# Layer 1's first stage: k of tiles 2 to 15 and q of six of them by seven block products per pair of token tiles

## The chip, the cores and the metric

One Trainium2 chip, one of its cores. The metric is the device time of one execution in microseconds; the median of the runs of a kernel counts. All arithmetic is fp32, done on TensorE in three passes: each operand is split into a high part (rounded to fp32r) and a low part (the rest), and high x high, high x low and low x high are added in PSUM.

## The reference

Two layers, each an attention block and a feed-forward block, on x of 2048 tokens by 640:

```python
def _A_ref(x, wqkv, wo):            # 32 heads of 20
    q, k, v = ...                   # x @ wqkv
    phi = lambda t: jnp.where(t > 0, t + 1, jnp.exp(t)) + 1e-6
    pq, pk = phi(q), phi(k)
    kv = jnp.einsum("bhsd,bhse->bhde", pk, v)
    z = jnp.einsum("bhsd->bhd", pk)
    num = jnp.einsum("bhqd,bhde->bhqe", pq, kv)
    den = jnp.einsum("bhqd,bhd->bhq", pq, z)[..., None] + 1e-6
    return (num / den) @ wo
...
for _ in range(2):
    x = x + _A_ref(_layernorm(x), wqkv, wo)
    x = x + _B_ref(_layernorm(x), w1, b1, w2, b2)   # relu(h) ** 2 between
```

phi can be written as min(exp(t), 1) + max(t, 0) + 1e-6, and both kernels compute it so.

## The kernel before, in words

Tokens come in 16 tiles of 128. A layer has three stages. The first, with which this case deals, takes each tile t through: load x and normalize it (`a_stats`, `a_apply`; the helper is `ln_stats`: two bn_stats and one bn_aggr on VectorE, then an add and a power on GpSimd for the reciprocal deviation rs; `ln_apply` on VectorE uses rs). Then x goes out to DRAM (`spread_out`, a DMA on GpSimd's queue), comes back with its blocks spread over the partitions (`spread_in`, four DMAs on SyncE's queue), and is transposed block by block on VectorE (`turn`) and split into high and low (`xT_split`). `part` multiplies the transposed x with columns of the k and q weights `kq` (five chunks of 128 rows, 15 matmuls for each block of columns, lines 660 and after); `Phi` evacuates with Exp on ScalarE (line 673) and two passes on VectorE (680, 681). k is split into high and low (`k_post`, 867 and 877) and added into `acc` by a DMA on GpSimd's queue. `g_part` (568) adds x^T k into five PSUM banks for the first 512 columns of k, `gt_part` (709) does the other 128 columns for a pair of tiles at a time, and VectorE adds its result into GT (711, 713). Plain tiles do k and q in blocks of 512, 512 and 256 columns. For six tiles, listed in `LATE`, only k is done in the stage, in two blocks of 320; q of these tiles follows in the second stage (`late_q`).

Three PSUM banks (`XB`) go round for these products, five hold G. The order is written out by hand, and each engine takes its instructions strictly in that order, waiting for semaphores where data isn't there.

Beside the stage, layer 1 also prepares sums of w1's blocks for the last group of the feed-forward block, which multiplies by seven products instead of eight: `sum_load` loads two blocks, `sum_ops` (four subtractions of 256 columns and two low parts on VectorE, line 920, two high parts on ScalarE, line 924) stores them to DRAM. Its steps are called one at a time from the tile loop.

The second stage makes M from G, v and wo; the third is the feed-forward block in four groups of 512 tokens. Layer 0's last group loads k and q's weights again (`load_kq`) and normalizes the first three tiles of layer 1, sends them out and back, and transposes two of them.

## Time and profile before

| | us |
|---|---|
| median of 3 runs | 1308.34 |
| lowest and highest | 1307.31, 1310.12 |
| span of the profiled execution, first to last instruction | 1306.4 |
| layer 1's first stage, in that execution | about 657 to 845 |

The profiled execution's own time is known by its span alone; 1.9 us lie between it and the median of the runs. The profile gives for each engine the busy time (PE is TensorE's matmuls, PEld its weight loads, DVE VectorE, ACT ScalarE, POOL GpSimd, SP SyncE, which only issues DMAs). The chain is followed back from the last instruction: at each step to what released it, or to the instruction before it on its engine; its shares say on whose time the end depends. A row of a group names line, engine, operation, what is written from what, shape and count, then busy time, mean ns, and the idle time just before with its releaser.

### The profile page before, as it was taken

What the parts mean: (1) busy time and instruction counts of PE and PEld (TensorE: products, weight loads), DVE (VectorE), ACT (ScalarE), POOL (GpSimd) and SP (SyncE); (2) the same over time, 40 slices, a digit from 0 to 9 for tenths busy, and PEclk for the clock granted to TensorE, in tenths of its full rate; (3) what the DMA queues carried; (4) which work ended last, traced back from release to release, by engine and by line L of the source; (5) the groups of instructions that cost most, each with busy time, mean ns of one, the idle gap of its engine ahead of it and who ended that gap; (6) DMA issues with size and microseconds to landing.
All of it is one profiled execution on the core that took longest, in us unless ns stands there. A gap on an engine that the chain in (4) does not pass through costs nothing.

```text
span 1306.4 us, 21586 instructions
## 1 busy us (share of the span) xinstructions
PE 1300.0 (100%) x7528; PEld 1188.3 (91%) x7528; DVE 971.1 (74%) x1811; ACT 746.3 (57%) x1662; POOL 239.6 (18%) x304
## 2 busy tenths in 40 slices
PE   9999999999999999999999999999999999999998
PEld 8888999989988988988988888999889899889998
DVE  8888968767965976933868777688869479569665
ACT  5888958785485486324323333397935934944342
POOL 2333310064031102101012222002420030021000
PEclk9999999999999999999999999999999999999999
DMA  6898985699997986998968666555999779779976
GB/s 195 252 278 269 310 262 171 255 354 385 320 336 252 322 331 237 302 369 285 346 214 237 207 173 176 145 183 195 327 329 340 283 253 335 294 249 315 358 267 222
DMA packets 155858, 357.02 MB, mean 273 GB/s; under 512 B 18454, under 2 KB 77718, under 8 KB 155110
## 3 DMA queue, kind: packets, MB, share of 16 engines
q1 hardware_dynamic: 148518, 333.36, 75.0%
q0 software_dynamic: 7232, 22.29, 6.6%
q8 instruction: 60, 0.98, 0.3%
q14 instruction: 48, 0.39, 0.1%
HBM read 267.72 MB, written 76.02 MB: 263 GB/s over the span
## 4 chain that ended last, share of the span: by engine, by line
PE 93%; DVE 3%; DMA 2%; ACT 1%; issue 0%; POOL 0%; SPq 0%; POOLq 0%
PE PS L1604 26%; PE PS L1360 23%; PE PS L660 20%; PE PS L568 10%; PE PS L1816 5%; PE PS L1476 3%; PE PS L709 2%; PE PS L595 1%; PE PS L1203 1%; PE PS L1191 1%; DMA u<-kept_m 1%; PE PS L982 1%; ACT z L534 1%; DMA kept_m<-arena 1%; ACT z L556 0%
## 5 line engine op out<-in xcount | busy, mean ns | idle before, releaser
L1360 PE MATMUL PS<-xTb,u 128*128 128x512 f32 x1490 | 346.1, 390 | 0.0
L1360 PEld LDWEIGHTS PS<-xTb,u 128*128 128x128 f32 x1490 | 277.8, 188 | 55.8 <-issue 0.2
L660 PE MATMUL PS<-kq,xT 128*128 128x320 f32 (+2 forms) x1575 | 283.8, 334 | 0.0
L660 PEld LDWEIGHTS PS<-kq,xT 128*128 128x128 f32 x1575 | 250.4, 188 | 27.2 <-DVE rl L681 1.0
L1604 PE MATMUL PS<-u,arena 128*128 128x320 f32 x1644 | 250.8, 309 | 0.0
L1604 PEld LDWEIGHTS PS<-u,arena 128*128 128x128 f32 x1644 | 243.4, 188 | 0.6
L534 ACT ACTIVATE z<-y 32x160 f32<-32x160 f32 x504 | 168.3, 334 | 35.1 <-DVE y L521 29.2
L1576 ACT ACTIVATE arena<-R 128x512 fp32r<-128x512 f32 (+1 forms) x200 | 114.9, 591 | 115.5 <-PE PS L1604 75.8
L1585 DVE TENSOR_TENSOR arena<-R,arena 128x512 fp32r<-128x512 f32 (+1 forms) x200 | 136.3, 688 | 41.3 <-ACT arena L1576 39.4
L568 PE MATMUL PS<-kh,xh 128*128 128x512 f32 x480 | 124.4, 393 | 0.0
L1371 ACT ACTIVATE R<-PS,b1sb 128x512 f32<-128x512 f32 x94 | 64.6, 687 | 95.5 <-PE PS L1360 94.7
L455 POOL TENSOR_SCALAR rs<-mv 128x1 f32<-128x1 f32 x63 | 30.6, 485 | 472.5 <-DVE mv L453 471.8
L1604 PE MATMUL PS<-uw,arena 128*128 128x320 f32 x660 | 106.1, 309 | 0.0
L568 PEld LDWEIGHTS PS<-kh,xh 128*128 128x128 f32 x480 | 87.3, 188 | 15.2 <-DVE xT L584 0.2
L1604 PEld LDWEIGHTS PS<-uw,arena 128*128 128x128 f32 x660 | 99.1, 188 | 0.3 <-DVE x L1618 0.2
L1550 DVE TENSOR_TENSOR R<-R 128x512 f32<-128x512 f32 (+1 forms) x128 | 86.7, 679 | 5.9 <-ACT R L1372 5.9
L556 ACT ACTIVATE z<-y 32x160 f32<-32x160 f32 x260 | 86.9, 334 | 4.9 <-DVE y L538 1.9
L673 ACT ACTIVATE r<-PS 128x512 f32<-128x512 f32 (+1 forms) x64 | 27.6, 433 | 88.4 <-PE PS L660 81.8
L1827 DVE TENSOR_TENSOR x<-PS,x 128x320 f32<-128x320 f32 x64 | 31.0, 489 | 61.7 <-PE PS L1816 59.1
L1618 DVE TENSOR_TENSOR x<-PS,x 128x320 f32<-128x320 f32 x112 | 53.1, 485 | 18.6 <-PE PS L1604 17.9
L1372 ACT ACTIVATE R<-R 128x512 f32<-128x512 f32 x94 | 59.5, 633 | 3.0
L680 DVE TENSOR_SCALAR r<-r 128x512 f32<-128x512 f32 (+1 forms) x64 | 21.2, 332 | 51.7 <-ACT r L673 51.5
(192 smaller groups left out, 1693.3 us busy)
## 6 DMA issues: line engine op xcount, KB each, us to landing
u<-kept SPq DMA_DIRECT2D x113, 640.0 KB
u<-kept_w SPq DMA_DIRECT2D x97, 640.0 KB
u<-kept SPq DMA_DIRECT2D x56, 320.0 KB
kept<-uprep SPq DMA_DIRECT2D x49, 320.0 KB
u<-kept_m SPq DMA_DIRECT2D x24, 640.0 KB
z<-xb SPq DMA_DIRECT2D x160, 80.0 KB
pqt<-pq SPq DMA_DIRECT2D x32, 320.0 KB
acc<-r POOLq DMA_DIRECT2D x28, 320.0 KB, 5.4
```

Of the source, the lines that this page charges most:

```text
L534: nc.scalar.activation(dst, blk, AF.Copy)
L556: nc.scalar.activation(dst, blk, AF.Copy)
L568: nc.tensor.matmul(ps, a, b, start=first and i == 0, stop=last and i == 2)
L660: nc.tensor.matmul(ps, xT[t][:, k, c, :], kq[c][:, l, a:b], start=(k, c, l) == seq[0], stop=(k, c, l) == seq[-1],)
L1360: nc.tensor.matmul(ps, a[:, d, :], bb[:, d, :], start=(d, i) == order[0], stop=(d, i) == order[-1],)
L1371: nc.scalar.activation(r, v, AF.Relu, bias=b1sb[:, c : c + 1])
L1372: nc.scalar.activation(r, r, AF.Square)
L1550: nc.vector.tensor_tensor(out=quad(*out, k), in0=quad(*x, k), in1=quad(*y, k), op=op)
L1576: nc.scalar.activation(u[:, 0], v, AF.Copy)
L1585: nc.vector.tensor_tensor(out=u[:, 1], in0=v, in1=u[:, 0].bitcast(F32), op=ALU.subtract)
L1604: nc.tensor.matmul(ps, x, y, start=opens and k == 0 and p == 0 and e == 0, stop=k == PAIRS - 1 and p == b - a - 1 and e == len(seq) - 1, s ...
L1816: nc.tensor.matmul(ps, x, y, start=m in (1, 5, 2, "d") and i == 0 and e == 0, stop=i == len(todo) - 1 and e == 2, skip_group_check=True,)
```

## The change

Layer 1's first stage is no longer done by the tile loop but by a new function, `paired_phase`. Layer 0's stage stays.

- Tiles 0 and 1 are done as plain tiles. From tile 2 on, two tiles a and b, two halves of the first 512 rows of the weights and two halves of their 640 columns make a product of 2 x 2 blocks, which takes seven products (`seven`, `product`) instead of eight; the last 128 rows are done plainly, 3 matmuls in each of four of the products. So k of a pair takes 54 matmuls of 320 columns instead of 60. q goes the same way in pairs 2, 3 and 5 (tiles 4 to 7, 10 and 11), in plain halves in pair 1, and late in pairs 4, 6 and 7.
- The products need sums of blocks of x (`sums_of_x`: four operations of 256 columns on VectorE, and high and low parts, per pair) and of the weights (`t_load` loads k's or q's weights once more, 20 DMAs on SyncE's queue; `t_sums` makes nine differences on GpSimd; `t_parts` the high and low parts: T13, T24 and TD in new tiles, T1 over two chunks of kq, which are loaded again for q by `reload_q` after pair 5).
- Products 1, 6, 7 and 4 accumulate in one bank, 5 and 3 in another, 2 in a third; after products 1, 6 and 5 ScalarE copies the bank as it stands, after 2, 7 and 3 VectorE adds it to such a copy.
- phi is now Exp and Relu on ScalarE and one pass on VectorE. Its epsilon is added apart: for k in the split and in zbc, for q by GpSimd before the store.
- The subtractions of w1's weight sums go from VectorE to GpSimd.
- A normalization is now one call, `x_norm`: statistics, apply and the DMA out.
- Layer 0's last group normalizes and spreads four tiles instead of three, and loads kq in the order of partitions that the unstrided `turn` gives, four DMAs a chunk instead of one. G's room is taken by the sums of x and phi's Exp during the stage.

The diff, cut to its core:

```diff
-LATE = ((9, 11, 12, 13, 14, 15), (8, 9, 11, 13, 14, 15))
+LATE = ((9, 11, 12, 13, 14, 15), (8, 9, 12, 13, 14, 15))
...
+QH = 2 * P
+Q_PAIRS = (2, 3, 5)
...
 def load_kq(c):
-        nc.sync.dma_start(kq[c].bitcast(F32), kept["kq", c])
+        for j in range(JQ):
+            nc.sync.dma_start(kq[c][j * B32 : (j + 1) * B32].bitcast(F32), rows_kq(c, j))
...
 def sum_ops(p):
             def sub(out, x, y, op=ALU.subtract):
-                nc.vector.tensor_tensor(out=out, in0=x, in1=y, op=op)
+                nc.gpsimd.tensor_tensor(out=out, in0=x, in1=y, op=op)
...
-        for t in range(NT):
+        for t in range(NT if layer == 0 else 0):
...
+def phi(dst, src):
+    e = slot(dst.shape[1])
+    nc.scalar.activation(e, src, AF.Exp)
+    nc.scalar.activation(dst, src, AF.Relu)
+    nc.vector.scalar_tensor_tensor(
+        out=dst, in0=e, scalar=1.0, in1=dst, op0=ALU.min, op1=ALU.add
+    )
+def q_store(t, rq):
+    nc.gpsimd.tensor_scalar(rq, rq, PHI_EPS, None, op0=ALU.add)
+    nc.sync.dma_start(pqd[t], rq)
+def k_split(t, r):
+    kh[t] = u = xtile("kh")
+    nc.scalar.activation(u[:, 0], r, AF.Identity, bias=eps1[:, 0:1])
+    if t == 0:
+        nc.gpsimd.tensor_copy(acc, r)
+    elif t < NT - 1:
+        nc.gpsimd.dma_start(acc, r, accum_op=ALU.add)
+    else:
+        nc.gpsimd.tensor_tensor(out=acc, in0=acc, in1=r, op=ALU.add)
+    nc.vector.scalar_tensor_tensor(
+        out=u[:, 1], in0=r, scalar=PHI_EPS, in1=u[:, 0].bitcast(F32), op0=ALU.add, op1=ALU.subtract
+    )
+def x_keep(t):
+    xh[t] = u = xtile("xh")
+    split(u[:, 0], u[:, 1], xt.pop(t))
+def x_norm(t):
+    if t < NT:
+        a_stats(t)
+        a_apply(t)
+        xb[t] = spread_out(xt[t])
+def x_load(t):
+    if t < NT:
+        zs[t] = spread_in(xb.pop(t))
+def x_turn(t):
+    if t >= NT:
+        return lambda: None
+    ys[t] = turn(zs.pop(t))
+    return xT_split(t, ys[t], True)
+def sums_of_x(a, b):
...
+    sub(y1[:, h1], y1[:, h0], y1[:, h1], ALU.add)
+    sub(y1[:, h0], y0[:, h0], y1[:, h0])
+    sub(y0[:, h0], y1[:, h1], y0[:, h0])
+    sub(y0[:, h1], y0[:, h1], y0[:, h0])
...
+def t_load(nm):
+    raw = [gtile("wt") for _ in range(DC)]
+    for c in range(DC):
+        for j in range(JQ):
+            w = wqkv[Q * j + B32 * c : Q * j + B32 * (c + 1), D * (nm == "k") :][:, :D]
+            nc.sync.dma_start(raw[c][j * B32 : (j + 1) * B32], w)
+    return raw
+def t_sums(raw):
+    def sub(out, x, y):
+        nc.gpsimd.tensor_tensor(out=out, in0=x, in1=y, op=ALU.subtract)
+    for c in range(2):
+        a, b = raw[c], raw[c + 2]
+        sub(a[:, rh], a[:, rh], a[:, lh])
+        sub(b[:, rh], b[:, rh], a[:, rh])
+        sub(b[:, lh], b[:, lh], b[:, rh])
+        sub(a[:, lh], b[:, rh], a[:, lh])
+    sub(raw[4][:, lh], raw[4][:, lh], raw[4][:, rh])
...
+def seven(nm, a, b, r, x, then):
...
+    step(1, pa)
+    copy(r[0][:, lh], pa)
+    step(2, pc)
+    add(r[0][:, lh], pc)
+    phi(r[0][:, lh], r[0][:, lh])
+    then.get(2, nothing)()
+    step(6, pa)
+    copy(r[0][:, rh], pa)
+    gs()
+    then.get(6, nothing)()
+    step(5, pb)
+    copy(r[1][:, rh], pb)
+    then.get(5, nothing)()
+    gs()
+    step(7, pa)
+    add(r[1][:, rh], pa)
+    step(3, pb)
+    add(r[0][:, rh], pb)
+    phi(r[1][:, rh], r[1][:, rh])
+    phi(r[0][:, rh], r[0][:, rh])
+    then.get(3, nothing)()
+    gs()
+    step(4, pa)
+    phi(r[1][:, lh], pa)
+    then.get(4, nothing)()
...
+k_split(1, r.pop(1))
+q_store(1, rqs.pop(1))
+gq += [(1, i) for i in range(DC)]
+x_norm(4)
+x_keep(2)
+x_norm(5)
+x_keep(3)
+x_load(4)
+x_load(5)
...
+for i in range(1, NT // 2):
+    a, b = 2 * i, 2 * i + 1
+    is_late = a in late
+    a_load(a + 4, src)
+    r = [rtile(), rtile()]
+    lows, work = {}, {}
+    if i == 1:
+        raw = t_load("q")
+    def k_2():
+        lows[0] = x_turn(a + 2)
+    def k_6():
+        lows[0]()
+        sum_step()
+    def k_5():
+        lows[1] = x_turn(b + 2)
+    def k_3():
+        lows[1]()
+        k_split(a, r[0])
+    def k_4():
+        work["sums"] = sums_of_x(a + 2, b + 2)
+    seven("k", a, b, r, X, {2: k_2, 6: k_6, 5: k_5, 3: k_3, 4: k_4})
+    a_load(b + 4, src)
+    if is_late:
+        gs(1)
+        gts(i - 1, 0, bank(X[2]))
+        k_split(b, r[1])
+        work["sums"]()
+        gs(2)
+        gts(i - 1, 1, bank(X[1]))
+        x_norm(a + 4)
+        sum_step()
+        if a + 2 < NT:
+            x_keep(a + 2)
+        x_norm(b + 4)
+        gs(2)
+        sum_step()
+        if b + 2 < NT:
+            x_keep(b + 2)
+        gs(DC * 2)
+        X = [X[2], X[0], X[1]]
+    elif i in Q_PAIRS:
+        X = [X[2], X[0], X[1]]
+        rq = [ftile("rq"), ftile("rq")]
+        def q_2():
+            k_split(b, r[1])
+            sum_step()
+            x_norm(a + 4)
+        def q_5():
+            x_norm(b + 4)
+        def q_3():
+            q_store(a, rq[0])
+            work["sums"]()
+            sum_step()
+        def q_4():
+            q_store(b, rq[1])
+        gs(1)
+        seven("q", a, b, rq, X, {2: q_2, 5: q_5, 3: q_3, 4: q_4})
+        gts(i - 1, 0, bank(X[2]))
+        gs(1)
+        x_keep(a + 2)
+        gts(i - 1, 1, bank(X[1]))
+        x_keep(b + 2)
+        gs(DC * 2)
+        X = [X[2], X[0], X[1]]
+        if i == Q_PAIRS[-1]:
+            for c in range(2):
+                reload_q(c)
+    else:
+        gs(1)
+        for n, t in enumerate((a, b)):
+            rq = ftile("rq")
+            for h in range(2):
+                ps = part(t, D + h * HD, D + (h + 1) * HD, bank(X[2 - h]))
+                phi(rq[:, h * HD : (h + 1) * HD], ps)
+                gs(1)
+                if (n, h) == (0, 0):
+                    k_split(b, r[1])
+                    x_norm(a + 4)
+                    if i == 1:
+                        t_sums(raw)
+                        t_todo = t_parts("q", raw)
+                elif (n, h) == (0, 1):
+                    work["sums"]()
+                    x_norm(b + 4)
+                elif i == 1:
+                    t_todo.pop(0)()
+            q_store(t, rq)
+            gts(i - 1, n, bank(X[0]))
+            x_keep((a, b)[n] + 2)
+            if i == 1:
+                t_todo.pop(0)()
+        for f in t_todo:
+            f()
+        t_todo = []
+        gs(DC * 2)
+        X = [X[2], X[1], X[0]]
+    gq += [(t, j) for t in (a, b) for j in range(DC)]
+    if i == 1:
+        sum_begin()
+    sum_step()
+    x_load(a + 4)
+    x_load(b + 4)
...
```

Three places show how instructions move. First VectorE's queue at the step from tile 1 to the next, where E is phi's Exp, xh the split of x for G, y the transposed x. Before:

```order
L451 BN_STATS bn<-xt 128x6 x2
L453 BN_AGGR mv<-bn 128x2
L877 TENSOR_TENSOR kh<-r,kh 128x640
L920 TENSOR_TENSOR uprep<-ws,uprep 128x512
L680 TENSOR_SCALAR rq<-rq 128x256
L681 SCALAR_TENSOR_TENSOR rq<-PS,rq 128x256
L463 TENSOR_SCALAR xt<-xt,mv,rs 128x640
L680 TENSOR_SCALAR r<-r 128x512
L681 SCALAR_TENSOR_TENSOR r<-PS,r 128x512
L510 STREAM_TRANSPOSE y<-z 128x4x5x32
```

Now:

```order
L1146 SCALAR_TENSOR_TENSOR kh<-r,kh 128x640
L465 BN_STATS bn<-xt 128x6 x2
L467 BN_AGGR mv<-bn 128x2
L477 TENSOR_SCALAR xt<-xt,mv,rs 128x640
L135 TENSOR_TENSOR xh<-xt,xh 128x640
L465 BN_STATS bn<-xt 128x6 x2
L467 BN_AGGR mv<-bn 128x2
L477 TENSOR_SCALAR xt<-xt,mv,rs 128x640
L135 TENSOR_TENSOR xh<-xt,xh 128x640
L1295 TENSOR_TENSOR r<-PS,r 128x320
L1129 SCALAR_TENSOR_TENSOR r<-E,r 128x320
L523 STREAM_TRANSPOSE y<-z 128x4x5x32
```

Other work used to stand between a tile's statistics and its apply (L463); now the apply (L477) follows at once, two normalizations stand in a row, and product 2's add (L1295) stands behind both.

Then VectorE's queue within a pair. Before, a plain tile's second half:

```order
L680 TENSOR_SCALAR r<-r 128x128
L681 SCALAR_TENSOR_TENSOR r<-PS,r 128x128
L680 TENSOR_SCALAR rq<-rq 128x384
L681 SCALAR_TENSOR_TENSOR rq<-PS,rq 128x384
L584 TENSOR_TENSOR xT<-y,xT 128x640
L1066 TENSOR_TENSOR xh<-xt,xh 128x640
L713 TENSOR_TENSOR GT<-PS,GT 128x320
L920 TENSOR_TENSOR ws<-st 128x256
L920 TENSOR_TENSOR ws<-ws,st 128x256
```

Now, q's seven products of pairs 2, 3 and 5:

```order
L1295 TENSOR_TENSOR rq<-PS,rq 128x320
L1129 SCALAR_TENSOR_TENSOR rq<-E,rq 128x320
L1146 SCALAR_TENSOR_TENSOR kh<-r,kh 128x640
L942 TENSOR_TENSOR st<-st,so 128x512
L465 BN_STATS bn<-xt 128x6 x2
L467 BN_AGGR mv<-bn 128x2
L477 TENSOR_SCALAR xt<-xt,mv,rs 128x640
L465 BN_STATS bn<-xt 128x6 x2
L467 BN_AGGR mv<-bn 128x2
L477 TENSOR_SCALAR xt<-xt,mv,rs 128x640
L1295 TENSOR_TENSOR rq<-PS,rq 128x320 x2
```

Between the add of product 2 (first row) and those of products 7 and 3 (last row) now stand k's low half, a weight sum's low half and both normalizations of the pair.

Last, GpSimd's queue, where wt are q's weights loaded for the sums. Before, around a tile:

```order
L491 DMA xb<-xt 128x640
L872 DMA acc<-r 128x640
L455 TENSOR_SCALAR rs<-mv 128x1
L458 TENSOR_TENSOR rs<-rs,neghalf 128x1
L491 DMA xb<-xt 128x640
```

Now, in pair 1:

```order
L1143 DMA acc<-r 128x640 x2
L469 TENSOR_SCALAR rs<-mv 128x1
L472 TENSOR_TENSOR rs<-rs,neghalf 128x1
L505 DMA xb<-xt 128x640
L1206 TENSOR_TENSOR wt<-wt 128x320 x9
L469 TENSOR_SCALAR rs<-mv 128x1
L472 TENSOR_TENSOR rs<-rs,neghalf 128x1
L505 DMA xb<-xt 128x640
L1134 TENSOR_SCALAR rq<-rq 128x640 x2
```

The nine differences stand between the rs of pair 1's first and second normalization.

More of the change, by code (lines that the diff above doesn't have):

```diff
@@ L881, in x_begin @@
         def x_begin(t):
[L882 removed]
+            yza[t] = blocks_x(xt[t])
         def x_end(t):
[L885 removed]
+            return yza.pop(t)[1]
         def move(t, n=JQ):
```

260 lines of the change are left out of this document (213 added, 47 removed).

## The prediction

> **What bounds the kernel now.** I read the page first, then the table of stretches, the chain of waits, and the groups by form inside the stage that is rebuilt. Of the page, the engines' busy times and the chain by engine:
>
> ```profile
> PE 1300.0 (100%) x7528; PEld 1188.3 (91%) x7528; DVE 971.1 (74%) x1811; ACT 746.3 (57%) x1662; POOL 239.6 (18%) x304
> PE 93%; DVE 3%; DMA 2%; ACT 1%; issue 0%; POOL 0%; SPq 0%; POOLq 0%
> ```
>
> TensorE never rests, and the chain runs along it. The stage is the stretch from 657 to 845 us (columns: stretch, its length, then busy time and count of PE, PEld, DVE, ACT, POOL, clock, DMA share, GB/s):
>
> ```profile
> 657.00:845.00 188.00, 188.00 (x1010) 165.98 (x1009) 136.99 (x271) 63.02 (x117) 40.90 (x55) 1.00 0.67 189
> ```
>
> TensorE is busy for all 188 us at full clock; VectorE has 51 us free, ScalarE 125, GpSimd 147. The chain in that stretch (start, length, what) gives the real pace of matmuls, which the groups' means, being of overlapping instructions, don't:
>
> ```profile
> 678.30 3.40 PE PS L660 x15
> 686.46 0.88 PE PS L709 x6
> 688.03 1.79 PE PS L660 x15
> 689.82 0.70 PE PS L568 x3
> 765.37 4.39 PE PS L660 x30
> ```
>
> Fifteen matmuls of 512 columns take 3.40 us, fifteen of 256 take 1.79, thirty of 320 take 4.39 (0.146 each); three of G take 0.70, six of GT 0.88. So fewer matmuls shorten the kernel at this pace, as long as nothing else becomes late.
>
> **What the change saves.** A plain tile costs 3.40 + 3.40 + 1.79 = 8.59 us, a pair 17.18. Seven products are 7 x 6 matmuls of 320 columns and 3 more in four of them for the fifth chunk of rows, 54 in all, 7.90 us. Where k and q both go so, a pair takes 15.80, 1.38 less; k alone 7.90 against 60 matmuls, 8.78, 0.88 less. Pairs 1 to 7 before: three plain pairs 51.54, tiles 8 and 9 with late q 8.78, pairs 5 and 6 (one plain, one late tile) 12.98 each, pair 7 8.78; together 95.06. After: pair 1 (k by seven, q by 60 plain) 16.68, pairs 2, 3 and 5 47.40, pairs 4, 6 and 7 23.70; together 87.78. Six tiles' late q stand on both sides. **Saved: 7.3 us.** Only 0.6%, so every wait that is added counts.
>
> **What the change adds on the other engines.** Their prices, VectorE first (line, engine, operation, tiles, shape, count, busy us, mean ns, idle before):
>
> ```profile
> L877 DVE TENSOR_TENSOR kh<-r,kh 128x640 fp32r<-128x640 f32 x16 | 13.7, 859 | 0.1
> L1066 DVE TENSOR_TENSOR xh<-xt,xh 128x640 fp32r<-128x640 f32 x16 | 13.1, 819 | 0.0
> L451 DVE BATCH_NORM_STATS2 bn<-xt 128x6 f32<-128x320 f32 x26 | 11.4, 482 | 0.0
> L463 DVE TENSOR_SCALAR xt<-xt,mv,rs 128x640 f32<-128x640 f32 x13 | 7.9, 608 | 2.8 <-POOL rs L458 2.8
> L713 DVE TENSOR_TENSOR GT<-PS,GT 128x320 f32<-128x320 f32 x14 | 6.6, 484 | 2.6 <-PE PS L709 2.6
> L681 DVE SCALAR_TENSOR_TENSOR r<-PS,r 128x320 f32<-128x320 f32 x12 | 5.9, 492 | 0.4
> L920 DVE TENSOR_TENSOR uprep<-ws,uprep 128x512 fp32r<-128x512 f32 x5 | 3.3, 669 | 0.0
> L920 DVE TENSOR_TENSOR ws<-st 128x256 f32<-128x256 f32 x5 | 2.0, 409 | 0.0
> L453 DVE BATCH_NORM_AGGREGATE mv<-bn 128x2 f32<-128x12 f32 x13 | 2.7, 209 | 0.4
> L521 DVE STREAM_TRANSPOSE y<-pqt 128x640 f32<-128x640 f32 x32 | 27.0, 844 | 1.0
> ```
>
> ScalarE and GpSimd:
>
> ```profile
> L867 ACT ACTIVATE kh<-r 128x640 fp32r<-128x640 f32 x16 | 11.9, 741 | 8.0 <-DVE r L681 8.0
> L673 ACT ACTIVATE r<-PS 128x320 f32<-128x320 f32 x12 | 5.2, 430 | 22.9 <-PE PS L660 22.9
> L491 POOL DMA_DIRECT2D xb<-xt x13 | 8.3, 637 | 17.0 <-DVE xt L463 13.9 <-DVE r L680 3.1
> L305 POOL TENSOR_TENSOR wq<-wb,wa 128x320 f32<-128x320 f32 x5 | 5.6, 1119 | 0.0
> L305 POOL TENSOR_TENSOR wq<-wa 128x320 f32<-128x320 f32 x5 | 4.4, 872 | 0.0
> ```
>
> And what a normalization costs VectorE when its apply stands right behind its statistics. From the timeline of before (start, length):
>
> ```profile
> 766.25 0.21 DVE L453 BATCH_NORM_AGGREGATE mv<-bn 128x2 f32<-128x12 f32 x1
> 766.37 0.77 DVE L877 TENSOR_TENSOR kh<-r,kh 128x640 fp32r<-128x640 f32 x1
> 767.92 0.61 DVE L463 TENSOR_SCALAR xt<-xt,mv,rs 128x640 f32<-128x640 f32 x1 [0.77 <-POOL rs L458]
> ```
>
> From the aggregate's end (766.46) to the apply's start lie 1.46 us, the way over GpSimd's two small operations. Before, kh's low half stands in it. In the changed order nothing does, and VectorE takes its queue in order. One normalization then holds VectorE 0.91 + 0.21 + 1.46 + 0.61 = 3.2 us, two per pair.
>
> *Step 1, pairs 2, 3 and 5.* In q's seven products VectorE's queue holds, between its add of product 2 and that of product 7: phi (Exp and Relu on ScalarE, 2 x 0.43, then 0.49), k's low half behind its high half (0.74, then 0.86), a weight sum's low half 0.67, two normalizations 6.4, the add 0.48. With phi's last part beside the high half that is 0.48 + 0.86 + 0.74 + 0.86 + 0.67 + 6.4 + 0.48 = 10.5; means overlap by about 0.1 in each of 12 steps, so 9.3. TensorE fills this with products 6, 5, 7, 3 and three G parts: 0.88 + 0.88 + 1.32 + 1.32 + 2.1 = 6.5. Product 4 goes into product 7's bank and waits for that add. Stall 2.8, and the four sums of x ahead of the first add make it 3.4. Bounds 2 (steps overlap more) and 4.7 (means as they stand, plus the sums). **Three times: 10.2 (6 to 14).** Before, such a pair with ten G and two GT blocks took 25.9; it would take 24.6 without waits and 28 with this one. It is the order that costs: what VectorE sheds (phi's first pass, the weight sums' four operations) it sheds elsewhere in the queue.
>
> *Step 2, the entry into pair 1.* Behind tile 1's last block stand on VectorE: phi, k's low half, two normalizations and two low halves of x, then product 2's add, phi, a transpose; ScalarE copies product 6 only behind that transpose's high half, and product 7 waits for the copy. 0.86 + 0.49 + 0.74 + 0.86 + 6.4 + 1.64 + 0.48 + 0.86 + 0.49 + 0.84 + 0.74 + 0.43 = 14.8, by 12 overlaps 13.6. TensorE has G, products 1, 2, 6, 5 and two G parts, 6.1. Stall 7.5. Ahead of it SyncE loads k's weights once more. Its queue's rows:
>
> ```profile
> 657.89 1.14 SPq L1625 DMA_DIRECT2D x<-x x2
> 660.61 3.78 SPq L913 DMA_DIRECT2D st<-in_B_w_dram x8
> 674.55 1.78 SPq L500 DMA_DIRECT2D z<-xb x4
> ```
>
> Twenty loads at 0.47 behind the last stores (659.0) are out at 668.4; GpSimd's first three differences wait for the third chunk, T24's low half for them, and k's low half, which G needs, stands behind that: 1 to 1.5 us. Two high halves of sums of x, 512 wide, stand on ScalarE before that phi: by VectorE's 0.67, 1.3. **10 in all (6 to 13).**
>
> *Step 3, GpSimd's nine differences of q's weights.* They stand between the two normalizations of pair 1: 9 x 0.95 = 8.5 us. VectorE goes from one apply to the next in 0.64 + 8.5 + 1.46 + 0.61 = 11.2; behind it is the copy of GT's first half, whose bank the second GT block needs. TensorE is then in q's third block and has 1.3 of it, two G parts and the fourth block left, 4.9: stall 6.3 (3 to 9), I take 6.5. What comes next is late too: VectorE's queue of 7.6 us up to q's last low half (GT 0.48, xh 0.82, two T24 1.64, two phis 0.98, five 320-wide low halves 2.4, GT, xh 1.3) frees the buffers for eight loads of w1 (3.8), behind which SyncE issues z (1.8) for pair 2's transpose; with transpose, high half and copy (2.0) that is 15.2, against TensorE's 0.5 to the GT copy, 0.9, two G parts and 6.1, 8.9. Product 7 then waits 6.3 and z's landing, 6.5 (1 to 9). **13 (4 to 18).**
>
> *Step 4, pair 4,* whose q is late: from product 4's end: phi 1.35, four sums 1.6, GT 0.5, k's low half 0.9, two of 512 1.3, GT 0.5, two normalizations 6.4, 0.7, two low halves of x 1.6, pair 5's add 0.5, then 3.4 to the copy as in step 2; 18.7, by overlaps 17.5. TensorE has seven G, two GT blocks, products 1, 2, 6, 5 and two G, 11.9. **6 (3 to 8).** Pair 6 normalizes nothing and gets by. *Step 5:* in each k, product 7 waits for a copy behind a transpose, 0.65: **3 (0 to 6)** over five pairs.
>
> At nothing I cost these: the added issues in layer 0's last group (about 15, some 7 us of SyncE's time in 60; TensorE waits for none of its loads there, at most 1 if that cover goes); q's epsilon on GpSimd (one operation of 640 a tile, 1.7 to 2.2 by twice the 320-wide rows, and only stores wait); reloading q's columns, two pairs before late q reads them; ScalarE's second pass, as 22 operations of 320 (9.5), six of 640 (4.4) and four of 512 (2.6) make 16.5 of such a pair's 28 us.
>
> **Sum:** 10.2 + 10 + 13 + 6 + 3 = 42 (19 to 59) less 7.3: +35. The profiled execution spans 1306.4; the median 1308.3 is 1.9 above it, which I keep: 1306.4 + 35 + 1.9 = **1343**. Its bounds are 1320 and 1360.
>
> **Whether a stall costs more than itself.** At the kernel's start TensorE's first 24 transposes, after nothing, against the same shape later:
>
> ```profile
> 1.42 5.22 PE L721 MATMUL PS<-ident 128*128 128x128 f32 x24 [1.42 <-POOL ident masks.py:199]
> L467 PE MATMUL PS<-ident,xn 128*128 128x128 f32 x20 | 2.8, 272 | 0.0
> ```
>
> 0.218 us each against 0.14: 1.9 us lost after an idle time. If each of the four long stalls (entry, both of step 3, step 4) brings this back, 7.5 us are added. The Trainium skill (TensorE: Matmul & The Clock Gate, "HAM oscillation — how this bites in real kernels") has the rule that idle gaps above about 3.4 us drop the array to half its clock until it is busy again. No gap of this trace tests that; by it the four gaps would pay, the 3.4 us ones of step 1 hardly.
>
> **The rivals.** *Faster, 1301:* the queues' waits don't reach TensorE. It decides at one point: if VectorE gets from the add of product 2 to that of product 7 in under 6.5 us, product 4 never waits, and likewise at the entry. For it speaks VectorE's 51 us of rest; against it, that the two waits of 1.46 and the order are fixed. 1308.3 - 7.3 = 1301.
>
> *Only the entry and GpSimd's differences cost, 1318:* pairs 2 to 7 run at TensorE's pace and the stalls of steps 2 and 3 come at about three quarters of their size: 17 - 7.3 = +10. For it: these don't hang on 0.1 us overlaps.
>
> *The clock falls in the long stalls, 1351:* 1343 + 7.5. For it the start's row; against it, that G parts are spread between the stalls.
>
> *No change, within 0.2%:* small stalls that happen to equal 7.3; nothing speaks for it.
>
> **How the numbers follow.** Forecast 0.56, clock rival 0.15, the 1318 rival 0.10, faster 0.15, no change 0.04. Within 0.2% (2.6 us, about what a measurement here can tell) is 0.04, faster 0.15, slower 0.81. The range leaves out the faster case: from 1310, under the 1318 rival, to 1361, the forecast's upper bound and the clock rival's middle.
>
> **What would show it.** Right: TensorE idle 35 to 50 us in the stage, released by VectorE's adds and ScalarE's copies at L1292 and L1295; VectorE waiting about 1.4 us for rs before most applies of xt; one wait of 8 to 10 us for rs in pair 1. Wrong: TensorE's idle time there under 10 us, or the stage (657 to 845) shorter than 188 us; then steps 1 to 4 fail together. Idle time with another releaser (DMA z, S) would leave the size and move the cause.

## The result, and the profile after

| | before | after |
|---|---|---|
| median of the runs beside each other, us | 1307.92 | 1398.80 |
| lowest, highest | 1307.31, 1310.12 | 1397.34, 1399.92 |
| span of the profiled execution | 1306.4 | 1395.6 |

The change makes the kernel slower: ratio 1.0691, 95% interval 1.0676 to 1.0706, 91 us. "Slower" was forecast, but by 35 us; the time lies far above the range.

The page of after, engines' busy times, and TensorE's and its clock's row of the 40 slices (35 us each):

```profile
PE 1320.8 (95%) x7588; PEld 1209.2 (87%) x7588; DVE 994.2 (71%) x1825; ACT 794.9 (57%) x1772; POOL 286.6 (21%) x354
...
PE   9999999999999999998867886799999999999999
...
PEclk9999999999999999999987898899999999999999
```

TensorE, which never rested, has a hole of eight slices in the middle, and the granted clock falls in five of them. Layer 1's first stage runs from the first matmul of tile 0 to the matmul of `acc` with ones. One row for it of before and one of after (stretch, length, busy time and count of PE, PEld, DVE, ACT, POOL, clock, DMA share, GB/s):

```profile
657.47:838.09 180.62, 180.62 (x972) 159.55 (x970) 133.50 (x264) 58.72 (x109) 40.90 (x55) 1.00 0.68 191
```

```profile
666.07:928.62 262.55, 199.66 (x1032) 179.61 (x1030) 155.39 (x274) 105.84 (x218) 85.47 (x100) 0.86 0.50 145
```

The stage starts 8.6 us later; this much is lost ahead of it, where in layer 0's last group TensorE waits 5.2 us for u. It takes 81.9 us longer: TensorE stands idle for 62.9 (262.55 - 199.66) and is busy for 19.0 more. It has more matmuls (1032 against 972), as blocks of 320 columns stand where 512 and 256 stood, but at the pace of before its products of k and q would take 7 us less. From the stage's end to the kernel's end it is 467.0 us, against 468.3. 8.6 + 62.9 + 19.0 - 1.3 = 89.2, the difference of the spans. No other engine is near its limit (VectorE is busy for 155 of 262 us), so the waits must come from what stands ahead of what in the queues, or from the hand-offs between engines; the experiments try the two against each other. What TensorE waits for in the stage (line waited for: us in total, times, longest):

```profile
PE PS L1270 <- ACT r L1292: 35.4, 7, 8.9
PE PS L723 <- DVE GT L725: 8.3, 1, 8.3
PE PS L1270 <- DVE rq L1295: 8.2, 3, 2.7
PE PS L1270 <- ACT rq L1128: 2.7, 2, 1.4
PE PS L581 <- DVE kh L1146: 2.3, 1, 2.3
PE PS L1270 <- ACT rq L1292: 2.1, 3, 0.9
```

More than half is one kind of wait, 34.7 us in six pairs: k's product 7, whose bank ScalarE has not yet copied out (line 1292 is the copy in `seven`). How that comes about in pair 4, from the timeline (start, length):

```profile
809.74 2.32 POOL L1134 TENSOR_SCALAR rq<-rq 128x640 f32<-128x640 f32 x1 [1.84 <-DVE rq L1129]
812.09 0.32 SPq L1135 DMA_DIRECT2D pq<-rq  x1
812.50 3.83 SPq L927 DMA_DIRECT2D st<-in_B_w_dram  x8
816.42 0.38 SPq L1135 DMA_DIRECT2D pq<-rq  x1
816.91 3.75 SPq L514 DMA_DIRECT2D z<-xb  x8
820.97 0.84 DVE L523 STREAM_TRANSPOSE y<-z 128x640 f32<-128x640 f32 x1 [2.66 <-DMA z<-xb]
821.85 0.74 ACT L594 ACTIVATE xT<-y 128x640 fp32r<-128x640 f32 x1 [4.06 <-DVE y L523]
822.49 0.42 ACT L1292 ACTIVATE r<-PS 128x320 f32<-128x320 f32 x1
822.96 0.85 PE L1270 MATMUL PS<-t,S 128*128 128x320 f32 x4 [3.61 <-ACT r L1292]
```

Read it backwards: TensorE waits for a copy; the copy stands on ScalarE behind the high part of the next pair's x; that waits for VectorE's transposition, and this for z to land. z was written out from 804.56 and 807.26 on (`spread_out`), but its loads stand on SyncE's queue behind q's store, which waits for GpSimd's epsilon, and behind eight loads of w1. Of this chain product 7 needs the copy alone.

### The profile page after: what moved, and what is told of

Its sections match the earlier page's. It is cut to its first block, busy times and chain, and to the rows that moved or that the text cites. A ratio compares the mean times of both kernels' runs of the same rounds, so it can differ in the third digit from the quotient of the medians.

```text
span 1395.6 us, 22049 instructions
## 1 busy us (share of the span) xinstructions
PE 1320.8 (95%) x7588; PEld 1209.2 (87%) x7588; DVE 994.2 (71%) x1825; ACT 794.9 (57%) x1772; POOL 286.6 (21%) x354
## 5 line engine op out<-in xcount | busy, mean ns | idle before, releaser
L674 PE MATMUL PS<-kq,xT 128*128 128x320 f32 (+2 forms) x1095 | 194.4, 332 | 2.0 <-DMA wt<-in_A_wqkv_dram 2.0
L674 PEld LDWEIGHTS PS<-kq,xT 128*128 128x128 f32 x1095 | 172.4, 189 | 19.6 <-issue 2.6
L547 ACT ACTIVATE z<-y 32x160 f32<-32x160 f32 x504 | 168.3, 334 | 35.1 <-DVE y L534 29.2
L581 PE MATMUL PS<-kh,xh 128*128 128x512 f32 x480 | 130.9, 403 | 2.9 <-DVE kh L1146 2.3
L469 POOL TENSOR_SCALAR rs<-mv 128x1 f32<-128x1 f32 x63 | 24.5, 390 | 464.6 <-DVE mv L467 463.7
L1270 PE MATMUL PS<-t,S 128*128 128x320 f32 x120 | 28.0, 363 | 37.5 <-ACT r L1292 35.4
L1270 PEld LDWEIGHTS PS<-t,S 128*128 128x128 f32 x120 | 22.4, 225 | 41.8 <-ACT r L1292 38.3
```

The costliest lines, as they stand in the source:

```text
L547: nc.scalar.activation(dst, blk, AF.Copy)
L581: nc.tensor.matmul(ps, a, b, start=first and i == 0, stop=last and i == 2)
L674: nc.tensor.matmul(ps, xT[t][:, k, c, :], kq[c][:, l, a:b], start=(k, c, l) == seq[0], stop=(k, c, l) == seq[-1],)
```

## The experiments

Two theories were tried against each other. *Order:* TensorE's waits come from what stands ahead of copies and additions in the queues of ScalarE, VectorE, GpSimd and SyncE, above all the way of the next pair's x. *Lockstep:* the hand-offs of phi (addition on VectorE, Exp and Relu on ScalarE, combination on VectorE) set the pace of a pair, and order is secondary. All runs are compared with the kernel before on the same chip; times are medians of four runs. Differences from the changed kernel ("after", 1398.8) go across chips, on which the kernel before took 1307.9 to 1308.4.

### One cause at a time

**`e2_tsums_after`**: GpSimd's nine differences of q's weights behind the second normalization of pair 1 instead of between the two.

```diff
                                 x_norm(a + 4)
-                                if i == 1:
-                                    t_sums(raw)
-                                    t_todo = t_parts("q", raw)
                             elif (n, h) == (0, 1):
                                 work["sums"]()
                                 x_norm(b + 4)
+                                if i == 1:
+                                    t_sums(raw)
+                                    t_todo = t_parts("q", raw)
```

> The changed kernel with GpSimd's nine differences of q's weights moved behind pair 1's second normalization. Theory: VectorE's wait of 6.6 us for rs and TensorE's of 8.3 us for the copy of GT go; as high and low parts come later by that much, some 3 us come back at pair 2; time 1390 to 1394. Rival: the parts of q's weights, the loads of w1 and z behind them are then the late ones, and pair 2's product 7 waits as much longer; time within 2 us of 1399.

Measured: 1401.2 us, ratio 1.0708 (1.0683 to 1.0733): nothing gained. TensorE's waits from there on, in the timeline of after and then of this run:

```profile
736.38 1.97 PE L723 MATMUL PS<-xh,kh 128*128 128x320 f32 x6 [8.27 <-DVE GT L725]
739.65 1.97 PE L1270 MATMUL PS<-kq,xT 128*128 128x320 f32 x6 [1.30 <-ACT rq L1128]
743.07 2.77 PE L1270 MATMUL PS<-kq,xT 128*128 128x320 f32 x9 [1.45 <-DVE GT L725]
753.07 0.86 PE L1270 MATMUL PS<-t,S 128*128 128x320 f32 x4 [2.72 <-ACT r L1292]
```

```profile
729.76 1.14 PE L723 MATMUL PS<-xh,kh 128*128 128x320 f32 x6 [1.58 <-DVE GT L725]
735.22 1.97 PE L1270 MATMUL PS<-kq,xT 128*128 128x320 f32 x6 [4.32 <-ACT rq L1128]
741.12 2.77 PE L1270 MATMUL PS<-kq,xT 128*128 128x320 f32 x9 [3.94 <-DVE GT L725]
754.35 1.43 PE L1270 MATMUL PS<-t,S 128*128 128x320 f32 x4 [6.25 <-ACT r L1292]
```

The wait for GT falls from 8.27 to 1.58 us, as the mechanism says, but the three that follow, 1.30, 1.45 and 2.72 in after, become 4.32, 3.94 and 6.25: 9.0 us come back. So it went as the rival said, within 0.2 us of its range.

**`e3_z_first`**: z's eight loads are issued earlier: behind the second normalization where q is late, behind q's first store in pairs 2, 3 and 5, and in every pair ahead of w1's loads. Of q's stores only the second stands behind them now. The diff shows pairs 2, 3 and 5, then the old place:

```diff
                         q_store(a, rq[0])
                         work["sums"]()
+                        x_load(a + 4)
+                        x_load(b + 4)
                         sum_step()
...
                 sum_step()
-                x_load(a + 4)
-                x_load(b + 4)
```

> The changed kernel with each pair's loads of the spread x put ahead of the stores of q, the loads of w1 and the second loading of q's columns in SyncE's queue. Theory: product 7 of k in pairs 3 to 6 waits 3.3, 3.6, 8.9 and 8.1 us because VectorE's transpose waits for this load; these fall to about 1 each, pair 5's to about 5 (VectorE is late there by itself): some 16 us of waits and some 5 of slow clock less, time about 1378. Rival: VectorE's own queue is the bound; only pair 6 gains, time about 1390.

Measured: 1400.5 us, 1.0703 (1.0683 to 1.0722), in neither range. Product 7's wait in pair 3 falls from 3.25 to 0.86 us, but product 3, 4 us later in the same pair, now waits for the copy of product 5, whose bank it takes:

```profile
787.59 0.72 POOL L935 TENSOR_TENSOR ws<-st 128x256 f32<-128x256 f32 x1 [7.91 <-DMA st<-in_B_w_dram]
789.15 0.63 ACT L940 ACTIVATE so<-ws 128x512 fp32r<-128x512 f32 x1 [3.00 <-POOL ws L935]
789.68 0.42 ACT L1292 ACTIVATE r<-PS 128x320 f32<-128x320 f32 x1
790.16 1.17 PE L1270 MATMUL PS<-kq,S 128*128 128x320 f32 x3 [2.38 <-ACT r L1292]
```

The loads of w1 are late instead; ScalarE's high part of w1's sums waits for them, and the copy stands behind it. Over pairs 2 to 6 the waits at product 7 fall from 26.6 to 9.4 us, so z's late arrival was most of their cause; those at product 3, of which after has none, come to 17.0. One wait out, another in.

**`e5_z3_late`**: in layer 0's last group, the load of tile 3's z is put 13 steps later, behind the last loads of u.

```diff
-                at(g, 10 + t if t < 3 else s + 14, lambda t=t: load(t))
+                at(g, 10 + t if t < 3 else s + 27, lambda t=t: load(t))
```

> The changed kernel with one edit: tile 3's spread x is loaded at the last step of layer 0 instead of 13 steps earlier. In the changed kernel's profile the stage starts at 666.1 us, 8.6 later than before, with a wait of 5.2 us for a load of w2 and one of 2.0 for kq. Theory: these four loads stand 6.3 us long in SyncE's queue and hold up the w2 and kq loads behind them; then the 5.2 us wait goes, the stage starts near 659 and the kernel takes about 1391. Rival: the transfer engines are simply full there (share 1.04), by the kq loads in four pieces; then the wait stays and the time stays within 2 us of 1399.

Measured: 1400.9 us, 1.0707 (1.0686 to 1.0729). TensorE still waits 7.2 us for u in that group; the load of z alone is not the cause there.

**`e4_fill_waits`**: TensorE does idle transposes of the identity, into unused columns of a bank, where it waited, to keep its clock up.

```diff
+            def fill(n, i):
+                for _ in range(n):
+                    nc.tensor.transpose(PS[:, 512 * i + HD : 512 * i + HD + P], ident, ident)
...
+                if nm == "k":
+                    fill({1: 52, 2: 14, 3: 18, 4: 20, 5: 56, 6: 52}.get(a // 2, 0), x[2])
                 step(7, pa)
...
+                if nm == "q":
+                    fill(16, x[2])
                 step(4, pa)
```

> The changed kernel with idle transposes into unused PSUM columns ahead of product 7 of k (52, 14, 18, 20, 56, 52 in pairs 1 to 6) and of product 4 of q (16), a little shorter than TensorE's waits there. They compute nothing that is used. Theory: of the 91 us, 63 are waits and 26 the lower granted clock (0.74 to 0.94 in the stage's stretches) after them; with TensorE kept busy the clock stays near 1 but for the wait for GT, and the time falls by 12 to 22, to about 1380. Rival: the clock column only mirrors the idle time and costs nothing; time within 3 us of 1399, or above it by what the transposes overrun.

Measured: 1397.7 us, 1.0682 (1.0666 to 1.0698). Pair 3, from the row of products at its start to that of pair 4, in after and with the fill (columns as above):

```profile
778.12:813.83 35.71, 29.40 (x151) 26.88 (x150) 22.02 (x41) 15.55 (x32) 11.67 (x14) 0.86 0.48 139
```

```profile
779.83:814.61 34.78, 29.34 (x185) 26.82 (x185) 21.88 (x41) 15.30 (x33) 11.69 (x14) 1.00 0.49 144
```

At full clock, and with 34 more (idle) matmuls within the same busy time, the pair takes 0.9 us less. Over the stage the granted clock rises from 0.86 to 0.94, and the kernel's time stays where it was. TensorE's slowness in the holes is real (29.40 us at clock 0.86 is 25.3 at 1.00), but where these gaps were filled it does not set the pace: faster products only wait longer. There the fall of the clock is a consequence.

### The way of x left out, or moved

**`e6_no_x_path`** leaves out, for tiles 6 to 15, normalization, spreading, transposition, parts and sums of x; every product, copy, addition and phi stays.

```diff
             def x_norm(t):
-                if t < NT:
+                if t < 6:
...
-                if t >= NT:
+                if t >= 6:
+                    if t < NT:
+                        xT[t] = xT[4 + t % 2]
                     return lambda: None
```

> Leaves out the way of x for tiles 6 to 15 in layer 1's first stage: their normalization, spreading, 32x32 transposition, high and low part and the sums of x (products then use tile 4's and 5's x). All products, copies, additions, phi and the sums of weights stay. If TensorE waits because the copies and additions that release its banks stand behind the steps of x in the queues of ScalarE and VectorE (theory: order), k's product 7 no longer waits from pair 2 on, nor q's product 4, and 35 to 50 us of waits with the lower clock that follows them go: 1330 to 1350 us. If the chain addition, exponential, Relu, combination of phi with its hand-offs between the two engines sets the pace of a pair (theory: lockstep), pairs keep some 33 to 35 us and the time stays above 1380.

Measured: 1350.5 us, 1.0314 (1.0277 to 1.0351), 48 us below after, just past the edge of what order expected and against lockstep. The same pair 3:

```profile
771.09:796.33 25.24, 25.10 (x151) 23.12 (x150) 11.91 (x23) 13.11 (x28) 8.31 (x9) 1.00 0.52 146
```

The same 151 matmuls take 25.24 us, TensorE's own pace. Phi with all its hand-offs is still there, so lockstep alone does not make 35.7. What stays in this run is mostly ahead of pair 3, where x still has its way: 8.0 us at pair 1's product 7, 4.0 for GT, and 8.5 in layer 0's last group.

**`e7_turn_late`**: transposition and high part of the next pair's x behind k's products 3 and 4 instead of 2 and 5; the sums of x follow in the second half.

```diff
-                def k_2():
-                    lows[0] = x_turn(a + 2)
...
                 def k_3():
-                    lows[1]()
                     k_split(a, r[0])
+                    lows[0] = x_turn(a + 2)

                 def k_4():
-                    work["sums"] = sums_of_x(a + 2, b + 2)
+                    lows[0]()
+                    lows[1] = x_turn(b + 2)
...
```

> One thing moved: the transposition of the next pair's z (VectorE) and its high part (ScalarE) are issued behind k's products 3 and 4 instead of 2 and 5, the sums of x follow in the second half of the pair; nothing is left out. Theory order: k's product 7 finds its bank copied out, so of 35.4 us of waits for the copies of products 6 and 5 at most 8 are left and the time falls to 1350 to 1370. Rival lockstep: the waits move to k's product 4 and q's products, pairs keep 34 to 36 us, 1390 to 1400.

Measured: 1409.8 us, 1.078 (1.0761 to 1.0799): slower than the change itself, so this expectation of order failed. The waits for copies of k fell (35.4 to 11.6), but the additions of GT hold TensorE up more (line 725's by 5.0, line 727's by 12.0), and q's product 6 now waits 3.6 to 4.5 us in three pairs:

```profile
801.92 0.84 DVE L523 STREAM_TRANSPOSE y<-z 128x640 f32<-128x640 f32 x1
802.79 0.74 ACT L594 ACTIVATE xT<-y 128x640 fp32r<-128x640 f32 x1 [1.65 <-DVE y L523]
805.36 0.83 DVE L523 STREAM_TRANSPOSE y<-z 128x640 f32<-128x640 f32 x1
806.23 0.74 ACT L594 ACTIVATE xT<-y 128x640 fp32r<-128x640 f32 x1 [2.05 <-DVE y L523]
806.87 0.42 ACT L1292 ACTIVATE rq<-PS 128x320 f32<-128x320 f32 x1
807.34 0.90 PE L1270 MATMUL PS<-t,S 128*128 128x320 f32 x2 [4.54 <-ACT rq L1292]
```

z is there now (VectorE does not wait for it), yet ScalarE waits for VectorE's transposition twice, and the copy stands behind both. So here it isn't enough that z comes in time: the step of x stands ahead of the copy, and waits for what VectorE's queue holds. That much of lockstep is true, that a hand-off between two in-order queues costs what the giver's queue holds.

**`c2_turn_and_sums_late`** adds the edit of `e2_tsums_after` to this.

> The move of the run before, and GpSimd's nine differences of q's weights behind pair 1's second normalization. Theory order: also the 8.3 us wait for GT in pair 1 goes and this time does not come back as a wait for z in pair 2, which now has the slack: 6 to 14 us below the run with the turn alone, 1338 to 1360. Rival lockstep: within 3 us of it and above 1385.

Measured: 1412.5 us, 1.0797 (1.0776 to 1.0818): missed too. GT's wait halves (13.3 to 6.8), and the next two products wait 7.3 instead of 2.8.

### Several causes at once

**`c3_four_moves`**: the edits of `e2_tsums_after`, `e3_z_first` and `e5_z3_late`; the step of w1's sums that comes behind product 6 goes behind product 4; and in a normalization the statistics are issued earlier, so that other work of VectorE lies over GpSimd's two operations:

```diff
                     def q_2():
+                        a_stats(a + 4)
                         k_split(b, r[1])
                         sum_step()
-                        x_norm(a + 4)

                     def q_5():
-                        x_norm(b + 4)
+                        x_norm(a + 4)
+                        a_stats(b + 4)
```

> Turns stay where the change has them, but all that delays them or stands beside them is moved: z's loads ahead of w1's and of q's stores, the sums of w1 from behind product 6 to behind product 4, the nine differences later, the statistics of a normalization apart from its application, layer 0's last z load later. Theory order: the waits for ScalarE's copies fall from 35 to under 15, that for GT from 8.3 to under 2, q's product 4 from 8.2 to about 3: 1345 to 1370. Rival lockstep: pairs keep 33 to 35 us, 1390 to 1400.

Measured: 1373.3 us, 1.0494 (1.0478 to 1.0510): 25.5 us below after, 3 us over order's range and far from lockstep's. Three of the five edits gave nothing one by one. The other two, the step of w1's sums and the earlier statistics, were not run alone, so the runs don't say how much of the gain is theirs; they do take away what `e3_z_first` ran into, and the wait of q's product 4. TensorE's waits in the stage:

```profile
PE PS L1269 <- ACT r L1291: 15.6, 7, 6.7
PE PS L1269 <- ACT rq L1291: 6.6, 3, 2.8
...
PE PS L1269 <- DVE rq L1294: 0.2, 1, 0.2
```

The copies of k fall from 35.4 to 15.6, nearly as expected, and q's product 4 from 8.2 to 0.2, of which q's product 7 takes back 4.5 (2.1 to 6.6). GT's additions now hold up product 2 of pairs 2 and 5, 4.0 and 3.9 us.

**`c4_x_behind_copies`**: more of the same kind: ScalarE's high part of x behind the copies of products 6 and 5, q's weights loaded and subtracted in the first half of pair 1, tiles 4 and 5 normalized earlier, the sums of x and GT's addition each later or earlier by one place.

```diff
                 def k_2():
-                    lows[0] = x_turn(a + 2)
+                    x_turn(a + 2)
...
                 def k_5():
-                    lows[1] = x_turn(b + 2)
+                    lows[0] = x_high(a + 2)
+                    x_turn(b + 2)
```

> The four moves of c3_four_moves (without the later differences) and five more: ScalarE's high part of x issued only behind the copies of products 6 and 5, the sums of x in the second half of a pair by seven products, the normalization of tiles 4 and 5 some 8 us earlier, the load and the nine differences of q's weights in the first half of pair 1 instead of beside its normalizations, GT's second addition of late pairs ahead of the sums of x. Nothing is left out. Theory order: of c3's remaining waits the entry's (6.7 us at product 7), those at the first two products of pairs 2 and 5 (3.5, 4.0, 3.9) and most of q's product 7 (6.6) go: 12 to 25 us below c3_four_moves, 1348 to 1362. Rival lockstep: the gain of c3 was all there is, 1370 to 1378.

Measured: 1357.3 us, 1.0382 (1.0359 to 1.0406): 41.5 us below after by order alone, as order expected. Pair 3 now takes 29.3 us, at full clock:

```profile
757.65:786.92 29.27, 25.50 (x152) 23.07 (x150) 21.77 (x41) 15.38 (x32) 14.03 (x15) 1.00 0.59 171
```

### Single parts

**`e8_kq_one_load`**: k's and q's weights by one transfer a chunk in layer 0's last groups, as before the change. It leaves out the order of rows that layer 1's products need, so it stands for the time alone.

```diff
-        for j in range(JQ):
-            nc.sync.dma_start(kq[c][j * B32 : (j + 1) * B32].bitcast(F32), rows_kq(c, j))
+        nc.sync.dma_start(kq[c].bitcast(F32), kept_kq[:, c])
```

> In layer 0's last groups, each of the five chunks of k's and q's weights comes by one transfer over 128 partitions again, instead of four over 32 partitions each; bytes are the same, but the rows then don't stand in block order, so layer 1's products k and q use permuted rows of the weights. Theory transfers: the 7 us that TensorE waits for u<-kept in layer 0's last group, and the 8.6 us by which the stage starts later, come from these 20 transfers on SyncE's queue: the start goes back by 5 to 9 us, 1390 to 1394. Rival: they come from the loads of z, and the time stays within 3 us of the change.

Measured: 1390.8 us, 1.0630 (1.0611 to 1.0650), 8.0 us below after, and the stage starts at 659.7 instead of 666.1. The same 30 us of layer 0's last group in after and here:

```profile
625.00:655.00 30.00, 25.44 (x172) 24.94 (x170) 21.50 (x39) 11.17 (x19) 0.00 (x0) 0.97 0.99 267
```

```profile
625.00:655.00 30.00, 29.13 (x196) 28.44 (x195) 22.65 (x42) 12.33 (x21) 0.00 (x0) 1.00 0.93 331
```

With four transfers of 32 partitions each, the DMA engines are busy for 0.99 and move 267 GB/s; with one of 128 they move 331 at 0.93. So the loads of u, which share the engines, come late. The run does not part the bytes from the 15 issues that it saves SyncE; that the engines are full at 0.99 and move less speaks for the bytes. The Trainium skill (DMA: Bandwidth & Descriptors, "Rules for kernel authors") asks for 128 partitions in a transfer, and says that two transfers to halves of the partitions share the same engines anyway; the rows, with quarters, agree, and put a price on it.

**`e9_phi_on_vector`**: Relu back from ScalarE to VectorE.

```diff
-                nc.scalar.activation(dst, src, AF.Relu)
-                nc.vector.scalar_tensor_tensor(
-                    out=dst, in0=e, scalar=1.0, in1=dst, op0=ALU.min, op1=ALU.add
-                )
+                nc.vector.tensor_scalar(e, e, 1.0, None, op0=ALU.min)
+                nc.vector.scalar_tensor_tensor(
+                    out=dst, in0=src, scalar=0.0, in1=e, op0=ALU.max, op1=ALU.add
+                )
```

> One part undone: Relu goes back from ScalarE to VectorE as two passes per part of phi (min of the exponential, then max and sum). 64 passes of some 0.47 us leave ScalarE, 64 join VectorE's queue, and one hand-off per part goes. Theory order: what counts is what stands in the queue ahead of the copies and additions; ScalarE's copies no longer stand behind Relu, VectorE's additions stand behind one pass more: within 10 us of the change, 1389 to 1409. Rival lockstep (the hand-offs set the pace): 20 us or more faster, under 1380. Rival VectorE as the bound: over 1420.

Measured: 1403.6 us, 1.0733 (1.0695 to 1.0772), not to be told from after. VectorE is busy for 170 us in the stage instead of 155, ScalarE for 85 instead of 106; neither shows in the time. The hand-off that goes here gives nothing back, which speaks against lockstep.

**`e10_k_only`**: `Q_PAIRS = ()`, and no load, differences, parts or reload of q's weights.

> One part alone: k by seven products as in the change, q of all pairs by plain products; no load, differences or parts of q's weights in block form, no reload. TensorE has 36 products of 320 columns more per pair of which q went back, three pairs, about 3 x 0.94 us. Theory order: the waits for GT in pair 1 (8.3), for q's product 4 (8.2) and part of product 7's go with what they delayed: 1368 to 1385. Rival lockstep: the pairs of q shrink by nothing, over 1390.

Measured: 1378.3 us, 1.0538 (1.0520 to 1.0555). Q by seven products and its preparation cost 20.5 us in all, for a saving of TensorE that the forecast's prices put at 2.6 (16.68 less 15.80, three times; six matmuls a pair, not the 36 of the expectation); the 35.1 us of waits for k's copies stay.

**`c5_k_only_moved`** joins `e10_k_only` with the moves of `c4_x_behind_copies` that concern x, w1 and GT; **`c6_k_only_one_load`** adds the edit of `e8_kq_one_load`.

> k by seven products, q plain in all pairs, with the moves of c4_x_behind_copies that concern x (load of z ahead of w1's, ScalarE's high part behind the copies, statistics apart, tiles 4 and 5 normalized earlier, GT's addition of late pairs earlier). Nothing is left out. Theory order: the run with k alone at 1378 had 35 us of waits for ScalarE's copies, of which these moves take 25 to 35: 1335 to 1352. Rival (a remainder of the seven products themselves, in lockstep or a longer time per matmul): it stays above 1357, where all of q's products by seven were kept.

> The run before, and each chunk of the weights by one load over 128 partitions, whose rows are then permuted. If the parts add up, it lies 6 to 10 us below the run before, 1326 to 1345: still 18 to 37 us above the kernel before, since waits at the stage's entry and at the pairs' edges stay while the whole saving of k's seven products is some 5 us. If it falls below 1308, seven products of k pay once the queues are in order, and the change failed by its order alone.

Measured: 1346.0 us, 1.0287 (1.0272 to 1.0303), and 1339.9 us, 1.0244 (1.0227 to 1.0261). Both lie in the expected ranges. c5 is the fastest version that leaves nothing out; none beats the kernel before. The stage of c6:

```profile
658.14:866.12 207.98, 185.46 (x1049) 167.95 (x1048) 146.71 (x258) 98.15 (x202) 83.53 (x91) 0.97 0.55 159
```

It starts where before does (657.5) and is 27.4 us longer: 22.5 idle, the rest busy. At full clock TensorE would need 180.6 less 4.6 for k's seven products (7.3 less the 2.6 of q), 176.0; divided by the clock of 0.97 that is 181.4, and 4 us of its busy time stay unexplained.

## Why the prediction was wrong

The direction held, and TensorE's waits end with lines 1292, 1295 and the copy of GT, as "what would show it" had it. But they come to 62.9 us and not 35 to 50, and behind much of them stands a late z, which the prediction named as the sign of another cause. Its terms against the profile of after:

| term of the sum | forecast | measured in after |
|---|---|---|
| step 1, q's product 4 in three pairs | 10.2 | 8.2 |
| step 2, entry into pair 1 | 10 | 13.0 (0.5, 2.3, 1.4, 0.7, 8.1) |
| step 3, GT in pair 1, then pair 2 | 6.5 + 6.5 | 8.3 + 5.5 |
| step 4, product 7 of pair 5 | 6 | 8.9 |
| step 5, product 7 of pairs 3, 4 and 6 | 3 (over five pairs) | 15.0 (3.25, 3.61, 8.14) |
| q's product 7; a load of the raw weights | 0 | 2.1 + 2.0 |
| all waits of the stage | 42 | 62.9 |
| TensorE's busy time | -7.3 | +19.0 |
| layer 0's last group | 0, at most 1 | 8.6 |

**Steps 1 to 4 were nearly right** in place, releaser and size. Step 2 came out at its upper bound and step 4 above it: in `e3_z_first`, with z earlier, step 4's wait is 6.2, so the forecast 6 is VectorE's part and the rest came from z. Step 3's second half fell on products 1, 2 and 7 of pair 2, not on product 7 alone. VectorE's wait for rs was 1.00 us an apply, not 1.46, and the long one 6.6, not 8 to 10.

**Step 5 failed, and with it "pair 6 normalizes nothing and gets by".** I let product 7 wait for a copy behind a transposition whose z was there, 0.65 us. z was not there. Its loads wait on SyncE behind q's stores, which wait for GpSimd's epsilon ("only stores wait" was the sentence that hid it), and behind eight loads of w1, 3.8 us of issue. I had priced these rows in step 3 for pair 2 and not asked for the other pairs, though the order is the same in each. In pair 6, x of tiles 14 and 15 still has to come in and be turned; that it normalizes nothing for later tiles frees VectorE, not SyncE. There the reload of q's columns, which I had also put at nothing, stands ahead of z's loads; VectorE then waits 6.67 us for z, and TensorE 8.14:

```profile
879.89 5.11 SPq L224 DMA_DIRECT2D kq<-kept_kq  x8
885.11 3.84 SPq L514 DMA_DIRECT2D z<-xb  x8
890.78 1.44 PE L1270 MATMUL PS<-t,S 128*128 128x320 f32 x4 [8.14 <-ACT r L1292]
```

`e6_no_x_path` shows that the way of x is what makes the pairs long, `e3_z_first` and `e7_turn_late` that neither z's arrival nor the place of the transposition alone mends it, and `c3_four_moves` and `c4_x_behind_copies` that several moves together give 25.5 and 41.5 us back.

**"At nothing" failed for layer 0's last group.** I counted SyncE's time for the added issues and not the bytes that the transfers could move: `e8_kq_one_load` gives back 6.4 of the 8.6 us at the stage's start, and 8.0 us of the median.

**The clock rival's mechanism came true, but its accounting misleads.** Of the busy time forecast, 173.3, the granted clock of 0.86 makes 201; 199.7 was measured, so 26 us of the table are slower matmuls. Adding them to the waits, as that rival did with 7.5, would suggest that a filled gap returns them. `e4_fill_waits` shows that it doesn't, for the gaps that it fills: while other engines set a pair's pace, a slow matmul eats idle time. So the queues hold TensorE up by more than its idle time says: pair 3 takes 34.8 us there at full clock, for products of 24.6 by the forecast. That is some 10 us, where steps 1 and 5 had 3.4 and 0.65. For the rule that I cited (the Trainium skill, TensorE: Matmul & The Clock Gate, "HAM oscillation — how this bites in real kernels": idle gaps over some 3.4 us halve the clock), the trace agrees after long gaps: after 8.27 us of idle six matmuls of 320 take 1.97 us, against 1.04. It shows no sharp bound: four take 1.44 us after a gap of 3.25, 1.43 after one of 2.73, and 0.85 after one of 3.61.

**The saving itself was nearly right.** With hardly anything in its way a pair with k and q by seven products takes 25.24 us (`e6_no_x_path`); I had 24.6, against 25.9 before. Two gaps of about 0.2 us, ahead of k's product 3 and q's product 7, make most of the difference. So the gain in reach was 7.3 us at most, and no rearrangement that leaves 22 us of waits can pay.

What stays open: whether an order without any wait exists for these buffers (in c5's stage TensorE still waits at fifteen places, 0.4 to 5.8 us each), how c3's gain divides among its edits, and the 4 us of TensorE's time in c6.

## What to carry to other kernels

When a block algorithm trades a few matmuls for more steps on other engines, follow every queue once for each repetition, SyncE's and GpSimd's too, and ask of every copy that frees a PSUM bank what stands ahead of it and what that waits for. Where in-order queues wait on each other, removing one wait only shows the next one; test the cause by taking a whole path out or by moving several things together, and do not conclude from single moves that gave nothing before you have seen where the time went instead. A lower clock and a lower busy share in the holes are symptoms until a run that restores them gives time back.

## What the runs showed of the hardware

A transfer split into four over 32 partitions each cost DMA bandwidth: 267 GB/s at a share of 0.99, against 331 at 0.93 with one over 128 partitions. The landing of z itself was no surprise, a median of 2.2 us from issue in the stage; it was the queue ahead of the issue, 3.8 us for eight loads. Idle transposes of the identity kept the granted clock up: 1.00 in pair 3 instead of 0.86. After 52 of them in pair 1 four matmuls of 320 columns took 0.83 us, where after the idle gap of 8.13 four took 1.44.
